# Attention's product with v in six parts, normalising one step later, and another order at its end

## The chip, the cores and the metric

The kernel runs on one core of one Trainium2 chip. A core has five engines that run at the same time, each through its own list of instructions in order: TensorE (PE in the profile, its weight loads PEld), VectorE (DVE), ScalarE (ACT), GpSimd (POOL), and SyncE (SP), which here only starts DMAs; ScalarE can start DMAs too. The metric is the device time of one execution in microseconds, as the median of several runs; lower is better.

## The reference

Attention with heads mixed before and after the softmax, and two dense blocks behind it:

```python
scores = scale * q @ k.T                                   # 4 batches, 12 heads, 448 x 448, depth 64
scores = einsum('bhij,hg->bgij', scores, w_pre)
attn = softmax(scores, axis=-1)                            # with + 1e-9 under the fraction
attn = einsum('bhij,hg->bgij', attn, w_post)
x = (attn @ v) as 1792 tokens x 768
x = ((x @ w1) * (x @ w2)) @ w3 @ w_out                     # 768 -> 1024 -> 1024 -> 768
out = relu(x @ w_in) ** 2 @ w_out2                         # 768 -> 2048 -> 768
```

The weights arrive as 64-bit numbers; those that are used must be turned into 32-bit ones on the chip.

## The kernel before

**Attention.** The queries of a batch are cut into four chunks (16 chunks `n` in all), a chunk into blocks of up to 10 queries times 12 heads (180 blocks `g`, `blocks`). The work goes in steps `d`, two blocks in each (`attention_step`). For a block: a DMA brings its scores together (`regroup`, tile `r`), two steps ahead; TensorE mixes the heads (`premix`, PSUM tile `sp`, two buffers); VectorE takes the row maximum (`rowmax`, tile `nm`); ScalarE the exponential and its sum (`expo`, tiles `p` and `sm`); GpSimd adds the small number to the sum (`norm_add`), VectorE inverts it (`norm_recip`); ScalarE writes the normalised upper half (`p_hi`, tile `ph`), VectorE the lower one (`p_lo`, tile `pl`); TensorE mixes the heads again (`tmix`, tile `tp`), two steps after `premix`; VectorE or ScalarE moves the result to `p2` (`p2_dve`, `p2_act`). When all blocks of a chunk are through, TensorE multiplies by v (`pv`, PSUM tile `pv`, one buffer) in two groups of 24 matmuls, ScalarE copies each result out (`pv_out`, tile `xs`), and a DMA stores it in `xd`. In the same steps the scores of the next chunk are made (`scores`, `evac`), and q and k are read and split in an upper and a lower part (`load_q`, `high_q`, `low_q`, `load_k`, `high_k`, `low_k`; k only at the start of a batch).

**What sets the order.** Nothing is scheduled by the compiler: instructions run on an engine as the code writes them. `attention_plan` gives the steps of scores, loads and `pv`; the tables `ORDER`, `NEEDS`, `LAG` and `AFTER` give the order inside a step and how many steps a kind lags behind `premix`.

**Weights ahead.** `Moe.ahead` turns 24 pieces of weights into 32 bits during attention: a load, a copy on ScalarE (`narrow`), three instructions on VectorE (`join`, tile `f`, lines 101, 103, 105), and a store. They are spread by a fixed period of three steps.

**The end of attention.** From step `closed` on there are no more scores; their memory is taken by the dense blocks. `tail_plan` reads the first eight weight pieces (`raw`) and x of the first batch (`xl`) and splits them (`wh`, `wl`, `xh`, `xl`); `early` gives TensorE the first matmuls of the dense blocks (`e`) between the last steps. `begin` and `Moe.step` read and split x of the second batch.

**Dense blocks.** Eight weight pieces lie ready at most, the others follow in a pipeline by pieces (`stage`: load, narrow, join, split); `mixed` is the order of the first units, `self.order` that of their matmuls. Pieces that were not turned ahead (`wide`) need the three joins here, and are stored again (`keep`).

## Time and profile before

| | us |
|---|---|
| runs shown | 1327.46, 1329.35, 1332.04 |
| median | 1329.35 |
| profiled execution | 1333.6 |
| its span | 1331.7 |
| until the first premix | 28.27 |
| first premix to the premix of step 83, the 84th | 402.27 |
| from there to the last wait of TensorE | 65.20 |
| from there to the end | 835.96 |

In a timeline row the first number is the start in microseconds, the second the length; `xN` is a number of instructions in one row, and brackets hold the idle time before and what ended it. A row of TensorE lasts until the result has left the array, so that rows overlap; what a step costs is read from start to start. The names are those of the tiles, without their numbers.

### The profile page before, as it was taken

What the parts mean: (1) busy time and instruction counts of PE and PEld (TensorE: products, weight loads), DVE (VectorE), ACT (ScalarE), POOL (GpSimd) and SP (SyncE); (2) the same over time, 40 slices, a digit from 0 to 9 for tenths busy, and PEclk for the clock granted to TensorE, in tenths of its full rate; (3) what the DMA queues carried; (4) which work ended last, traced back from release to release, by engine and by line L of the source; (5) the groups of instructions that cost most, each with busy time, mean ns of one, the idle gap of its engine ahead of it and who ended that gap; (6) DMA issues with size and microseconds to landing.
All of it is one profiled execution on the core that took longest, in us unless ns stands there. A gap on an engine that the chain in (4) does not pass through costs nothing.

```text
span 1331.7 us, 23506 instructions
## 1 busy us (share of the span) xinstructions
PE 1291.6 (97%) x8714; PEld 1117.5 (84%) x8714; DVE 839.9 (63%) x1414; ACT 727.0 (55%) x1558; POOL 469.6 (35%) x473
## 2 busy tenths in 40 slices
PE   6999999999999899999999999999999999999998
PEld 3667767776677579999999999999999999999998
DVE  4899889889888647585327785588345424801731
ACT  4878877887787644443323663574344434533530
POOL 4243234225211412200332232210468656734730
PEclk9999999999999899999999999999999999999999
DMA  5676567677564544565346764476321211121131
GB/s 182 199 207 218 158 211 221 194 196 229 171 177 138 168 127 123 159 207 158 107 147 204 253 205 148 136 209 237 105 74 55 72 60 42 66 72 37 57 98 58
DMA packets 109879, 196.03 MB, mean 147 GB/s; under 512 B 22405, under 2 KB 76677, under 8 KB 109317
## 3 DMA queue, kind: packets, MB, share of 16 engines
q1 hardware_dynamic: 93349, 176.86, 44.5%
q10 hardware_dynamic: 16416, 17.67, 3.7%
q8 instruction: 69, 1.13, 0.4%
q14 instruction: 45, 0.37, 0.1%
HBM read 120.18 MB, written 35.78 MB: 117 GB/s over the span
## 4 chain that ended last, share of the span: by engine, by line
PE 75%; issue 7%; ACT 6%; DVE 5%; DMA 4%; POOL 3%; SPq 0%; POOLq 0%; ACTq 0%; DVEq 0%
PE l L62 33%; PE y L62 9%; PE p L62 5%; PE sp L295 4%; PE tp L351 3%; PE pv L392 3%; ACT p L309 3%; PE sc L269 2%; DMA kraw<-k 1%; ACT ph L334 1%; POOL ql L252 1%; DVE p L366 1%; ACT s L280 1%; DVE nm L301 1%; POOL sm L324 1%
## 5 line engine op out<-in xcount | busy, mean ns | idle before, releaser
L295 PE MATMUL sp<-r,kpre 120*120 120x448 f32 x360 | 163.1, 575 | 14.1 <-ACT p L309 7.2
L309 ACT ACTIVATE p<-sp,nm 120x448 f32<-120x448 f32 x180 | 113.3, 637 | 73.1 <-DVE nm L301 72.1
L125 POOL TENSOR_TENSOR wl<-f,wh 128x384 fp32r<-128x384 f32 (+1 forms) x52 | 58.6, 1127 | 215.0 <-ACT wh L121 205.4
L351 PEld LDWEIGHTS <-ph 120*128 120x128 f16 (+1 forms) x1440 | 108.2, 99 | 30.7 <-issue 30.3
L324 POOL TENSOR_SCALAR sm<-sm 120x2 f32<-120x2 f32 (+3 forms) x94 | 29.5, 314 | 285.2 <-ACT p L309 282.2
L351 PE MATMUL tp<-kwh,ph 120*128 120x120 f16 x720 | 122.0, 219 | 4.5 <-ACT p L364 2.9
L301 DVE TENSOR_REDUCE nm<-sp 120x1 f32<-120x448 f32 x180 | 106.1, 618 | 27.4 <-PE sp L295 24.1
L341 DVE SCALAR_TENSOR_TENSOR pl<-p,sm,ph 120x448 f16<-120x448 f32 x180 | 122.7, 722 | 0.0
L334 ACT ACTIVATE ph<-p,sm 120x448 f16<-120x448 f32 x180 | 111.9, 683 | 18.2 <-DVE sm L329 17.9
L351 PE MATMUL tp<-kwh,pl 120*128 120x120 f16 x720 | 121.1, 218 | 0.0
L351 PE MATMUL tp<-kwl,ph 120*128 120x120 f16 x720 | 121.1, 218 | 0.0
L269 PE MATMUL sc<-kt,qh 128*110 128x448 f32 (+1 forms) x192 | 102.7, 535 | 9.8 <-DVE kt L230 8.3
L295 PEld LDWEIGHTS sp<-r,kpre 120*120 120x120 f32 x360 | 60.3, 188 | 59.0 <-issue 20.7
L280 ACT ACTIVATE s<-sc 110x448 f32<-110x448 f32 (+1 forms) x186 | 90.5, 554 | 14.2 <-PE sc L269 8.2
L366 DVE TENSOR_SCALAR p<-tp,iv 112x480 f32<-112x480 f32 (+1 forms) x135 | 90.9, 701 | 3.3 <-PE tp L351 3.2
L103 DVE SCALAR_TENSOR_TENSOR f<-y,f 128x384 int32<-128x384 int32 (+1 forms) x120 | 85.6, 713 | 4.1
L392 PE MATMUL pv<-p,v 112*64 112x110 f32 (+1 forms) x1536 | 80.7, 261 | 0.6 <-ACT xs L401 0.6
L269 PE MATMUL sc<-kt,ql 128*110 128x448 f32 (+1 forms) x192 | 76.1, 396 | 3.7 <-POOL ql L252 3.1
L105 DVE SCALAR_TENSOR_TENSOR f<-raw,f 128x384 int32<-128x384 int32 (+1 forms) x120 | 77.5, 646 | 3.3
L101 DVE TENSOR_SCALAR f<-y 128x384 int32<-128x384 int32 (+1 forms) x120 | 70.0, 583 | 14.4 <-ACT y L89 14.4
L392 PEld LDWEIGHTS pv<-p,v 112*64 112x64 f32 x1536 | 73.8, 137 | 4.0 <-ACT xs L401 0.8
L125 POOL TENSOR_TENSOR wl<-raw,wh 128x384 fp32r<-128x384 f32 (+1 forms) x36 | 44.2, 1231 | 92.1 <-ACT wh L121 92.1
(981 smaller groups left out, 3550.7 us busy)
## 6 DMA issues: line engine op xcount, KB each, us to landing
r<-s SPq DMA_DIRECT2D x172, 210.0 KB
raw<-w SPq DMA_DIRECT2D x32, 384.0 KB
raw<-win SPq DMA_DIRECT2D x32, 384.0 KB
raw<-wo SPq DMA_DIRECT2D x24, 512.0 KB
kraw<-k SPq DMA_DIRECT2D x22, 448.0 KB
raw<-w3t SPq DMA_DIRECT2D x16, 512.0 KB
qraw<-q SPq DMA_DIRECT2D x36, 220.0 KB
raw<-wo SPq DMA_DIRECT2D x16, 384.0 KB
```

Source lines behind the costliest of these rows:

```text
L62: nc.tensor.matmul(acc, w, x, start=(first and i == 0 and j == 0), stop=(last and i == n - 1 and j == 2), **kw)
L125: eng.tensor_tensor(self.out[i][1], self.ft.pop(i), f32(self.out[i][0]), ALU.subtract)
L269: nc.tensor.matmul(sc[:ic], t[:, hh * ic : hh * ic + ic], self.kt[b, h // 2][:, h % 2], start=(i == 0), stop=(i == 1))
L280: nc.scalar.activation(self.st[n][:ic, h], self.sc.pop((n, h))[:ic], AF.Copy)
L295: nc.tensor.matmul(t[:kk], self.kpre[:kk, :kk], self.rt.pop(g)[:kk], start=True, stop=True)
L301: nc.vector.tensor_reduce(nm[:kk], self.sp[g][:kk], AX.X, ALU.max, negate=True)
L309: nc.scalar.activation(p[:kk], self.sp.pop(g)[:kk], AF.Exp, bias=self.nm.pop(g)[:kk], accum_out=self.sm[g // 2][:kk, g % 2 : g % 2 + 1],)
L334: nc.scalar.activation(self.phl[g % NP][0][:kk, :S], self.pt[g][:kk], AF.Copy, scale=self.sm[g // 2][:kk, g % 2 : g % 2 + 1])
L341: nc.vector.scalar_tensor_tensor(l, self.pt.pop(g)[:kk], self.sm[g // 2][:kk, g % 2 : g % 2 + 1], h, ALU.mult, ALU.subtract)
L351: nc.tensor.matmul(t[:, j, :, :cnt], p[:kk, j * JP : j * JP + 128], w[:kk, :, :cnt], start=(i == 0), stop=(i == 2))
L366: nc.vector.tensor_scalar(d, t, self.iv[:JP], None, ALU.mult)
L392: nc.tensor.matmul(t[64 * e : 64 * e + 64, x, :ic], self.v[b][:, j, g], self.p2[n][:, j, g, :ic], start=(j == 0), stop=(j == JC - 1),)
```

## The change

`pv` is cut in six parts of 8 matmuls (`x` counts three of them to a group), spread over the steps until the next chunk is through, where before two groups of 24 stood in two steps; `pv_out` follows the third part of a group. `norm_recip` and `p_hi` lag one step; inside a step `p_hi` and `pv_out` stand first on ScalarE, `norm_recip` first on VectorE, and `p_lo` waits for `p_hi` of its step. `ahead` turns 20 pieces instead of 24, one join in a step, in steps that have no `high_k` and no `high_k` just before; `load_k` comes a step earlier, with three buffers. At the end: `p2_act` takes every second block; the loads of the first eight pieces and of x are started by ScalarE instead of SyncE; the lower halves of pieces and x are made by VectorE instead of GpSimd; x of the second batch is read and split earlier; the first matmuls of the dense blocks begin one block later. The first `l1` unit behind the early ones moves two pieces forward.

Two places on VectorE and ScalarE, in the middle of chunk 8. First VectorE before, from the row maximum of blocks 96 and 97 (`sm` numbers name the first block of a pair):

```order
L301 TENSOR_REDUCE nm96_3905<-sp96_3875 120x1
L301 TENSOR_REDUCE nm97_3907<-sp97_3877 120x1
L341 SCALAR_TENSOR_TENSOR pl2_93<-p94_3855,sm94_3854,ph2_92 120x448
L341 SCALAR_TENSOR_TENSOR pl3_95<-p95_3857,sm94_3854,ph3_94 120x448
L329 RECIPROCAL sm96_3911<-sm96_3911 120x2
L366 TENSOR_SCALAR p28_3863<-tp93_3892,iv_96 112x48x10
L245 CAST qh10_1_3921<-qraw10_1_3785 128x440
L301 TENSOR_REDUCE nm98_3977<-sp98_3937 120x1
L301 TENSOR_REDUCE nm99_3979<-sp99_3939 120x1
L341 SCALAR_TENSOR_TENSOR pl0_89<-p96_3912,sm96_3911,ph0_88 120x448
L341 SCALAR_TENSOR_TENSOR pl1_91<-p97_3914,sm96_3911,ph1_90 120x448
```

And the same place now:

```order
L329 RECIPROCAL sm94_3820<-sm94_3820 120x2
L301 TENSOR_REDUCE nm96_3883<-sp96_3844 120x1
L301 TENSOR_REDUCE nm97_3885<-sp97_3846 120x1
L341 SCALAR_TENSOR_TENSOR pl2_93<-p94_3821,sm94_3820,ph2_92 120x448
L341 SCALAR_TENSOR_TENSOR pl3_95<-p95_3823,sm94_3820,ph3_94 120x448
L366 TENSOR_SCALAR p28_3829<-tp93_3861,iv_96 112x48x10
L245 CAST qh10_1_3898<-qraw10_1_3755 128x440
L105 SCALAR_TENSOR_TENSOR f18_3835<-raw18_3602,f18_3835 128x384
L329 RECIPROCAL sm96_3889<-sm96_3889 120x2
L301 TENSOR_REDUCE nm98_3963<-sp98_3913 120x1
```

The reciprocal of a pair came behind its row maximum and the lower halves of the pair before; now it comes behind everything else of its step, ahead of the next row maximum. One join stands in a step.

ScalarE before, from the exponentials of blocks 94 and 95:

```order
L309 ACTIVATE p94_3855,sm94_3854<-sp94_3787,nm94_3848 120x448
L309 ACTIVATE p95_3857,sm94_3854<-sp95_3789,nm95_3850 120x448
L280 ACTIVATE s9_3493<-sc9_10_3791 110x448
L280 ACTIVATE s9_3493<-sc9_11_3794 110x448
L334 ACTIVATE ph2_92<-p94_3855,sm94_3854 120x448
L334 ACTIVATE ph3_94<-p95_3857,sm94_3854 120x448
L309 ACTIVATE p96_3912,sm96_3911<-sp96_3875,nm96_3905 120x448
L309 ACTIVATE p97_3914,sm96_3911<-sp97_3877,nm97_3907 120x448
L334 ACTIVATE ph0_88<-p96_3912,sm96_3911 120x448
L334 ACTIVATE ph1_90<-p97_3914,sm96_3911 120x448
L364 ACTIVATE p28_3863<-tp92_3879,iv_96 112x48x10
```

And now:

```order
L309 ACTIVATE p94_3821,sm94_3820<-sp94_3757,nm94_3811 120x448
L309 ACTIVATE p95_3823,sm94_3820<-sp95_3759,nm95_3813 120x448
L280 ACTIVATE s9_3457<-sc9_10_3761 110x448
L280 ACTIVATE s9_3457<-sc9_11_3764 110x448
L334 ACTIVATE ph2_92<-p94_3821,sm94_3820 120x448
L334 ACTIVATE ph3_94<-p95_3823,sm94_3820 120x448
L309 ACTIVATE p96_3890,sm96_3889<-sp96_3844,nm96_3883 120x448
L309 ACTIVATE p97_3892,sm96_3889<-sp97_3846,nm97_3885 120x448
L364 ACTIVATE p28_3829<-tp92_3848,iv_96 112x48x10
L89 ACTIVATE y20_3905<-raw20_3838 128x384
L334 ACTIVATE ph0_88<-p96_3890,sm96_3889 120x448
L334 ACTIVATE ph1_90<-p97_3892,sm96_3889 120x448
```

The order of exponential, copies and upper halves is kept; the copy of the mixed block (L364) and `narrow` (L89) now come ahead of the upper halves instead of behind them.

ScalarE at the end of attention before, from the upper halves of blocks 168 and 169:

```order
L334 ACTIVATE ph0_88<-p168_6658,sm168_6657 120x448
L334 ACTIVATE ph1_90<-p169_6660,sm168_6657 120x448
L364 ACTIVATE p214_6385<-tp164_6625,iv_96 112x48x10
L401 ACTIVATE xs13_1_6668<-pv13_1_6570 128x3x110
L665 ACTIVATE xh0_6533<-xl0_6534 128x6x110 x2
L309 ACTIVATE p170_6720,sm170_6719<-sp170_6683,nm170_6713 120x448
L309 ACTIVATE p171_6722,sm170_6719<-sp171_6685,nm171_6715 120x448
L334 ACTIVATE ph2_92<-p170_6720,sm170_6719 120x448
L334 ACTIVATE ph3_94<-p171_6722,sm170_6719 120x448
L121 ACTIVATE wh0_6731<-raw0_6612 128x384
L665 ACTIVATE xh0_6533<-xl0_6534 128x6x110
```

And at this end now, from the exponentials of blocks 166 and 167, with the DMA starts that ScalarE has taken from SyncE:

```order
L309 ACTIVATE p166_6549,sm166_6548<-sp166_6499,nm166_6539 120x448
L309 ACTIVATE p167_6551,sm166_6548<-sp167_6501,nm167_6541 120x448
L81 DMA raw0_6558<-w1f_60 128x384
L81 DMA raw1_6560<-w1f_60 128x384
L676 ACTIVATE xh0_6491<-xl0_6492 128x6x110
L334 ACTIVATE ph2_92<-p166_6549,sm166_6548 120x448
L334 ACTIVATE ph3_94<-p167_6551,sm166_6548 120x448
L309 ACTIVATE p168_6613,sm168_6612<-sp168_6567,nm168_6606 120x448
L309 ACTIVATE p169_6615,sm168_6612<-sp169_6569,nm169_6608 120x448
L364 ACTIVATE p214_6347<-tp164_6571,iv_96 112x48x10
L81 DMA raw2_6622<-w2f_61 128x384
L676 ACTIVATE xh0_6491<-xl0_6492 128x6x110
```

The split of x (`xh`) is spread over the steps, and each weight load and x load stands in ScalarE's list.

```diff
-        def load(self, i, src, wide):
+        def load(self, i, src, wide, eng=nc.sync):
             n = src.shape[1]
...
                 t = self.p.tile([128, PW, 2], I32, tag="raw", name=f"raw{i}", bufs=self.nraw)
-                nc.sync.dma_start(t[:, :n].rearrange("p n t -> p (n t)"), src.bitcast(I32))
+                eng.dma_start(t[:, :n].rearrange("p n t -> p (n t)"), src.bitcast(I32))
                 self.raw[i] = t[:, :n]
...
                 t = self.p.tile([128, PW], F, tag="raw", name=f"raw{i}", bufs=self.nraw)
-                nc.sync.dma_start(t[:, :n], src)
+                eng.dma_start(t[:, :n], src)
                 self.ft[i] = t[:, :n]
...
             else:
-                raw = self.ka.tile([128, 2, S], F, tag="kraw", name=f"kraw{b}_{r}", bufs=2)
+                raw = self.ka.tile([128, 2, S], F, tag="kraw", name=f"kraw{b}_{r}", bufs=3)
             nc.sync.dma_start(raw, k[b, :, 2 * r : 2 * r + 2])
...
         def p2_act(self, g):
-            if g % 4 == 0:
+            if g % (4 if g < first[15] - 4 else 2) == 0:
                 self.p2_evac(g, 0)
...
         def p2_dve(self, g):
-            if g % 4:
+            if g % (4 if g < first[15] - 4 else 2):
                 self.p2_evac(g, 1)
...
-        def pv(self, n, y):
+        def pv(self, n, y, x):
             b, c = divmod(n, 4)
...
             assert all(("p", z) in self.done for z in range(first[n], first[n + 1]))
-            t = self.pvt[n, y] = self.ps.tile([128, 3, IC], F, tag="pv", name=f"pv{n}_{y}", bufs=1)
-            for x in range(3):
-                for j in range(JC):
-                    for e in range(2):
-                        g = 6 * y + 2 * x + e
-                        nc.tensor.matmul(
-                            t[64 * e : 64 * e + 64, x, :ic], self.v[b][:, j, g], self.p2[n][:, j, g, :ic],
-                            start=(j == 0), stop=(j == JC - 1),
-                        )
-        def pv_out(self, n, y):
+            if x == 0:
+                self.pvt[n, y] = self.ps.tile([128, 3, IC], F, tag="pv", name=f"pv{n}_{y}", bufs=1)
+            t = self.pvt[n, y]
+            for j in range(JC):
+                for e in range(2):
+                    g = 6 * y + 2 * x + e
+                    nc.tensor.matmul(
+                        t[64 * e : 64 * e + 64, x, :ic], self.v[b][:, j, g], self.p2[n][:, j, g, :ic],
+                        start=(j == 0), stop=(j == JC - 1),
+                    )
+        def pv_out(self, n, y, x):
+            if x < 2:
+                return
             o, ic, _ = CHUNKS[n % 4]
...
                         add(t - 2, "high_q", n, h // 4)
-            for y in range(2):
-                add((first[n + 1] + 5 + (5 if n < 15 else 0) * y) // 2, "pv", n, y)
+            t0, t1 = (first[n + 1] + 5) // 2 + (n == 14), (first[n + 2] if n < 15 else 0) // 2 + 2
+            for z in range(6):
+                add(t0 + z * (t1 - t0) // 6 if n < 15 else t0, "pv", n, *divmod(z, 3))
         for b in range(1, B):
...
                 t = lo[4 * b] - 6 + 3 * r // 2
-                add(t - 1, "load_k", b, r)
+                add(t - 2, "load_k", b, r)
                 add(t, "high_k", b, r)
...
         ("premix", "scores", "tmix", "pv"),
-        ("expo", "evac", "p_hi", "p2_act", "pv_out"),
-        ("rowmax", "p_lo", "norm_recip", "p2_dve", "high_q", "high_k"),
+        ("p_hi", "pv_out", "expo", "evac", "p2_act"),
+        ("norm_recip", "rowmax", "p_lo", "p2_dve", "high_q", "high_k"),
         ("norm_add", "low_q", "low_k"),
...
     NEEDS = {
-        "rowmax": "premix", "expo": "rowmax", "evac": "scores", "norm_add": "expo", "norm_recip": "norm_add",
-        "p_hi": "norm_recip", "p2_act": "tmix", "p2_dve": "tmix",
+        "rowmax": "premix", "expo": "rowmax", "evac": "scores", "norm_add": "expo", "p_hi": "norm_recip", "p_lo": "p_hi",
+        "p2_act": "tmix", "p2_dve": "tmix",
     }
...
         "premix": 0, "tmix": 2, "p2_act": 2, "p2_dve": 2, "rowmax": 0, "expo": 0,
-        "norm_add": 0, "norm_recip": 0, "p_hi": 0, "p_lo": 1,
+        "norm_add": 0, "norm_recip": 1, "p_hi": 1, "p_lo": 1,
     }
...
             wop = [self.wo_piece(c, h) for c in range(8) for h in range(2)]
-            mixed, rest = l1[:4] + wop[:6], wop[6:]
+            mixed, rest = l1[:4] + wop[:4] + [l1[4]] + wop[4:6], wop[6:]
             for i in range(8):
-                mixed.append(l1[4 + i])
+                mixed += [l1[4 + i]] if i else []
                 for _ in range(1 + (i % 4 == 3)):
...
             self.at = [int(x) for x in n]
-            self.order = [None, (3, 0), (0, 1), None, (1, 1), None, (2, 1), None, (3, 1)]
-            for i in range(10, len(self.units)):
+            self.order = [None, (3, 0), (0, 1), None, (1, 1), None, (2, 1), None, (3, 1), (8, 0), (8, 1)]
+            for i in range(11, len(self.units)):
                 self.order += [(i, t) if self.units[i][1] else None for t in range(len(self.units[i][0]))]
...
-        def ahead(self, ka, n, start, period):
+        def ahead(self, ka, n, plan, last):
             w, ev = Weights(ka, PW, 2, 2, 2, 0, 0), {}
-            def at(d, f):
-                ev.setdefault(d, []).append(f)
+            keys = {d for d, x in plan.items() if "high_k" in x}
+            free = [d for d in range(1, last) if not {d, d - 1} & keys]
+            at = lambda d, f: ev.setdefault(d, []).append(f)
...
+            ends = [-9, -9]
             for j, i in enumerate([i for i, x in enumerate(self.pieces) if "keep" in x][:n]):
-                d, x = start + period * j, self.pieces[i]
-                at(d, lambda i=i, src=x["src"]: w.load(i, src, True))
-                at(d + 2, lambda i=i: w.narrow(i))
-                for part in range(3):
-                    at(d + 3 + part // 2, lambda i=i, part=part: w.join(i, part))
-                at(d + 6, lambda i=i, dst=x["keep"]: store(i, dst))
+                x, parts = self.pieces[i], [free[(3 * j + k) * len(free) // (3 * n)] for k in range(3)]
+                at(max(parts[0] - 5, ends[j] + 1), lambda i=i, src=x["src"]: w.load(i, src, True))
+                at(parts[0] - 1, lambda i=i: w.narrow(i))
+                for k, d in enumerate(parts):
+                    at(d, lambda i=i, k=k: w.join(i, k))
+                at(parts[2] + 2, lambda i=i, dst=x["keep"]: store(i, dst))
+                ends.append(parts[2])
                 self.pieces[i] = {"src": x["keep"], "wide": False}
...
-            for i in range(11):
-                t = 1 + i if i < 8 else 13 + i
-                at(t, lambda i=i: w.load(i, self.pieces[i]["src"], self.pieces[i]["wide"]))
-                if i == 8:
-                    at(t + 4, lambda i=i: w.narrow(i))
-                if i < 8:
-                    at(t + 4, lambda i=i: (w.place(i), w.high(i), w.rest(i)))
+            for i in range(8):
+                t = 2 * i if i > 3 else (1, 2, 4, 5)[i]
+                at(t, lambda i=i: w.load(i, self.pieces[i]["src"], False, nc.scalar))
+                at(2 * i + 5, lambda i=i: (w.place(i), w.high(i)))
+                at(2 * i + 7, lambda i=i: w.rest(i, nc.vector))
             for u in range(4):
-                at(u - 1, lambda u=u: self.load_x(u))
-                at(u + 3, lambda u=u: self.split_x(u))
+                at(u // 2 - 1, lambda u=u: self.load_x(u, nc.scalar))
+                at(2 * u + 2, lambda u=u: self.high_x(u))
+                at(2 * u + 4, lambda u=u: self.low_x(u, nc.vector))
             return ev
...
             self.load_x(4)
+            self.load_x(6)
+            for i in (8, 9, 10):
+                self.w.load(i, self.pieces[i]["src"], True)
+            self.w.narrow(8)
             slots = []
...
                     self.wot[c, h] = slots[4 * c + 2 * h], slots[4 * c + 2 * h + 1]
-            for u in (5, 6, 7):
-                self.load_x(u)
             for i in range(3):
...
         def step(self, p, it):
-            if p == 1:
+            if p == 0:
                 for u in range(4, 8):
-                    self.split_x(u)
+                    self.high_x(u)
+                    self.low_x(u, nc.gpsimd if u == 5 else nc.vector)
...
-        def load_x(self, u):
+        def load_x(self, u, eng=nc.sync):
             t, u4 = divmod(u, 4)
...
                 w = slice(CHUNKS[u4][0], sum(CHUNKS[u4 + 1][:2]))
-                nc.sync.dma_start(f32(self.xy["x", t][1][:, :, w]), xd[t, :, :, w])
-        def split_x(self, u):
+                eng.dma_start(f32(self.xy["x", t][1][:, :, w]), xd[t, :, :, w])
+        def x_rows(self, u):
             t, u4 = divmod(u, 4)
             o, ic, _ = CHUNKS[u4]
-            xh, xl = (x[:, :, o : o + ic] for x in self.xy["x", t])
+            return tuple(x[:, :, o : o + ic] for x in self.xy["x", t])
+        def high_x(self, u):
+            xh, xl = self.x_rows(u)
             nc.scalar.activation(xh, f32(xl), AF.Copy)
-            eng = nc.gpsimd if u < 4 or u == 5 else nc.vector
+        def low_x(self, u, eng):
+            xh, xl = self.x_rows(u)
             eng.tensor_tensor(xl, f32(xl), f32(xh), ALU.subtract)
...
         M, tail = Moe(), {}
-        ahead = M.ahead(ka, 24, 4, 3)
+        ahead = M.ahead(ka, 20, ev, closed - 3)
         for d in step:
...
                     a()
-                for _ in range(1 if g >= nb - 5 else 0):
+                for _ in range(1 if g >= nb - 4 else 0):
                     next(heads, None)
```

## Rows read from the trace of the kernel before

**Rows 1.** Windows, all engines: busy us (count) of each, granted clock, DMA share, GB/s; four stages.
```profile
0.00:28.27 28.27, 16.33 (x37) 9.04 (x37) 11.34 (x20) 13.81 (x21) 15.07 (x23) 1.00 0.55 176
28.27:430.54 402.27, 386.92 (x3923) 281.41 (x3923) 352.08 (x675) 320.88 (x760) 126.73 (x165) 0.99 0.66 195
430.54:495.74 65.20, 56.41 (x561) 44.15 (x558) 37.46 (x63) 35.66 (x79) 20.21 (x21) 0.92 0.50 147
495.74:1331.70 835.96, 831.95 (x4199) 782.92 (x4199) 439.05 (x658) 356.62 (x699) 307.61 (x264) 1.00 0.40 123
```

**Rows 2.** Timeline of TensorE, 209 to 240 us: start, length, instruction, count.
```profile
209.66 1.72 PE L295 MATMUL sp<-r,kpre 120*120 120x448 f32 x4
...
213.39 2.48 PE L392 MATMUL pv<-p,v 112*64 112x110 f32 x48
215.80 1.76 PE L295 MATMUL sp<-r,kpre 120*120 120x448 f32 x4
...
234.57 1.72 PE L295 MATMUL sp<-r,kpre 120*120 120x448 f32 x4
...
238.63 1.71 PE L295 MATMUL sp<-r,kpre 108*108 108x448 f32 x4
```

**Rows 3.** Timeline of TensorE around the last attention step with scores before it.
```profile
427.68 1.76 PE L295 MATMUL sp<-r,kpre 120*120 120x448 f32 x4
...
430.54 0.97 PE L295 MATMUL sp<-r,kpre 120*120 120x448 f32 x2
```

**Rows 4.** Waits in 28 to 430 us: who waited for whom, us in total, times, longest.
```profile
ACT p L309 <- DVE nm L301: 68.7, 51, 4.0
...
PEld sp L295 <- ACT p L309: 19.0, 39, 2.3
...
DVE sm L329 <- POOL sm L324: 9.4, 16, 1.5
...
PE sp L295 <- DMA r<-s: 2.7, 2, 1.8
```

**Rows 5.** Timeline of VectorE in one step, 210 to 216 us.
```profile
210.39 1.31 DVE L366 TENSOR_SCALAR p<-tp,iv 112x480 f32<-112x480 f32 x2
211.63 0.37 DVE L245 CAST qh<-qraw 128x440 fp32r<-128x440 f32 x1
211.92 0.61 DVE L221 CAST kt<-kraw 128x896 fp32r<-128x896 f32 x1
...
212.84 0.56 DVE L103 SCALAR_TENSOR_TENSOR f<-y,f 128x384 int32<-128x384 int32 x1
213.31 1.15 DVE L301 TENSOR_REDUCE nm<-sp 120x1 f32<-120x448 f32 x2
214.38 1.27 DVE L341 SCALAR_TENSOR_TENSOR pl<-p,sm,ph 120x448 f16<-120x448 f32 x2
```

**Rows 6.** Windows, 545 to 570 us, where the two weight pieces in question are used.
```profile
545.00:570.00 25.00, 24.73 (x124) 22.88 (x123) 16.00 (x28) 11.27 (x22) 5.05 (x5) 1.00 0.55 171
```

**Rows 7.** Windows, 434 to 442 us, while x is read back.
```profile
434.00:442.00 8.00, 5.63 (x82) 4.36 (x78) 5.04 (x10) 5.10 (x13) 0.59 (x2) 0.97 0.81 193
```

**Rows 8.** Timeline of all engines, 442 to 457 us; idle time before in brackets.
```profile
442.55 3.31 PE L295 MATMUL sp<-r,kpre 120*120 120x448 f32 x4 [2.92 <-DMA r<-s]
...
445.07 0.63 ACT L309 ACTIVATE p<-sp,nm 120x448 f32<-120x448 f32 x1 [1.11 <-DVE nm L301]
...
448.06 1.23 ACT L334 ACTIVATE ph<-p,sm 120x448 f16<-120x448 f32 x2 [0.77 <-DVE sm L329]
...
450.53 2.70 DVE L341 SCALAR_TENSOR_TENSOR pl<-p,sm,ph 120x448 f16<-120x448 f32 x2
...
456.04 0.17 DVE L329 RECIPROCAL sm<-sm 120x2 f32<-120x2 f32 x1 [2.82 <-POOL sm L324]
```

**Rows 9.** Timeline, 475 to 496 us: a DMA issue on ScalarE, and TensorE's last wait.
```profile
481.44 0.40 ACTq L403 DMA_DIRECT2D xd<-xs  x1
...
495.74 0.44 PE L62 MATMUL l<-xl,wh 128*128 128x448 f32 x1 [1.47 <-DVE xl L667]
```

## Prediction

> **What bounds the kernel now.** I read the windows by stage first, then the timeline of TensorE inside attention, then the waits, then the timeline of the end.
>
> The windows [rows 1] give four stages. In the last one, 835.96 us long, TensorE is busy for 831.95: it is the bound and nothing in this change gives it less to do. In attention up to step 83 (402.27 us) it is busy for 386.92, VectorE for 352.08, ScalarE for 320.88. That sum hides something: a row of TensorE lasts until its result has left the array, so I build the floor from starts. A step without scores or pv goes from 427.68 to 430.54, 2.86 us: two premix and 24 tmix [rows 3]. From 234.57 to 238.63 is 4.06, the same with six scores, so a score (two matmuls) costs (4.06 - 2.86)/6 = 0.20. From 209.66 to 215.80 is 6.14, with four scores and one pv group of 48 passes: 6.14 - 2.86 - 0.80 = 2.48 for the group, of which 2.41 would be its passes and 0.07 the seam, an estimate [rows 2]. Steps 0 to 82 hold, by the order, 81 steps with tmix, two without (1.6 each, estimate), 350 scores and 27 groups: 231.7 + 3.2 + 70.0 + 67.0 = 371.8. The trace needs 402.27, so 30.5 us are lost there.
>
> To whom? The only wait of TensorE named by the page itself is 2.7 us for a regrouped block and 19.0 for the exponential to free a premix buffer; the big row above them, the exponential waiting 68.7 us in 51 waits for the row maximum, points further back [rows 4]. The row maximum is VectorE's, and VectorE's list is in order. I counted its instructions in each step by the order and gave them the durations of [rows 5]: 0.575 for a row maximum, 0.635 for a lower half, 0.655 for a copy to `p2`, 0.37 and 0.61 for the casts of q and k, 0.56 for a join, and an estimate of 0.1 for the reciprocal. Over 83 steps that is 354 us against 373 of TensorE's passes, so on average VectorE keeps up; in 39 of the steps it doesn't, and what it has too much of in those sums to 33.9 us. Step 31 is an example: TensorE needs 2.86, VectorE 2 x 0.575 + 2 x 0.635 + 2 x 0.655 + 0.37 + 0.61 + 2 x 0.56 + 0.1 = 5.9. The step before has 6.17 of TensorE because it holds a pv group. Only two premix buffers stand between the engines, so little of an imbalance is carried over.
>
> The third stage [rows 1] is 65.20 us at a granted clock of 0.92. Its floor: seven steps of 2.86, 24 more tmix (2.5, estimate), five pv groups (12.4), 54 early matmuls at 0.20 (10.8) and 19 that the phase behind would else do (3.8), 49.8 in all; 15.4 are lost.
>
> **The change part by part.**
>
> *The middle.* The same count over the new order: step 31 has 3.75 of TensorE (one part of pv) and 2 x 0.575 + 2 x 0.635 + 2 x 0.655 + 0.37 + 0.61 + 0.1 = 4.8 of VectorE; the joins are gone from it. Over 83 steps VectorE falls to 348 us (four pieces fewer, 12 joins of 0.56), steps in which it has more than TensorE go from 39 to 24, and their overhang from 33.9 to 16.5: 51% of it goes. I apply that share to the loss less the 2.7 that is a DMA's: 27.8 x 0.51 = 14.2 less. Against it stand seams: the pieces of pv in these steps go from 27 to 68, 41 x 0.07 = 2.9 more. Sum -11.3. Bounds: none of the loss goes (+2.9), all of it goes (2.9 - 27.8 = -24.9). I take the share, since the count explains a loss of the size that the trace has (33.9 against 27.8).
>
> *Reciprocal and upper halves a step later.* The row "VectorE's reciprocal waits for GpSimd", 9.4 us in 16 waits, goes [rows 4]: the addition of GpSimd now has the rest of a step. What it brings is inside the sum above. What is queued behind: on ScalarE, in its list, the upper halves of a pair (1.23, [rows 8]) stand directly ahead of the next two exponentials, as before, but wait for a reciprocal that is now behind all else in VectorE's step. So the exponential starts no earlier than reciprocal + 1.23, and the second of a pair ends about 2.5 us after the reciprocal (1.23 + 2 x 0.63). TensorE needs the first buffer back a step later: 402.27/83 = 4.85 us before, some 4.7 by the sum above. VectorE needs 348/83 = 4.2 on average, so the reciprocal stands on average before the premix of its step is done, and TensorE's step hides it: cost 0. Without that cover it is rival A.
>
> *Copies at p2, key loads.* Counts of `p2_dve` and `p2_act` in the middle are the same; the third `kraw` buffer and an earlier issue can take only part of the loss that the joins beside key casts share. Counted above, nothing added.
>
> *The end.* Three of its losses have rows. Step 85's premix waits 2.92 for its block [rows 8] while the DMA engines are at 0.81 with x and weights [rows 7], and 442.55 to 448.06 takes 5.5 against 2.86, another 2.6, at the lower clock that follows the wait. Now ScalarE starts ten of these loads, so that SP's list holds the regroup alone, and x and weights come at other steps: I take half of the 5.5, -2.8, as the same bytes still move in the same few steps. VectorE waits 2.82 for GpSimd's addition, behind lower halves of x and weights on GpSimd [rows 8]; with these on VectorE that wait goes, and about 0.3 more of the chain behind it: -3.1. VectorE pays for it with eight lower halves of weights and seven of x, each about a microsecond or less at the rate of `pl` [rows 5]; its free time here is 65.20 - 37.46 = 27.7 us [rows 1]. And TensorE's last wait, 1.47 for `xl` of the second batch [rows 9], with 0.5 of small waits beside it: those splits come earlier now, -1.3 of the 2.0. Five parts of pv where two groups stood: +0.5 with the starts of DMAs on ScalarE (10 x 0.40, [rows 9], hidden in its 65.20 - 35.66 = 29.5 us of free time, but for one in front of an exponential). Sum -6.7. Bounds: nothing goes and all 4.0 of the starts lie on the path, +4; all of the lost 15.4 goes, -15.
>
> *The dense stage.* The four pieces that are no longer turned ahead cost it 12 joins, 12 x 0.56 = 6.7 us of VectorE, and four copies and four stores. They are `l1[10]` and `l1[11]`, used near 545 to 570; there VectorE is busy 16.0 of 25 us [rows 6], so 9 lie free under TensorE. I take +0.5; bounds 0 and +6.7. The stage as a whole is 835.96 and stays.
>
> *Sum.* -11.3 - 6.7 + 0.5 = -17.5. The profiled execution took 1333.6 (span 1331.7, 1.9 outside), 4.25 over the median of 1329.35; the sum is made on its own span and taken from the median: 1329.35 - 17.5 = 1312.
>
> The term for the block late in step 85 is one on which a page speaks. [Rows 7] show 0.81 of the DMA engines' time taken at that place. The Trainium skill, "DMA: Bandwidth & Descriptors", section "Issuing engines are not separate DMA queues", says that DMAs started from several engines land on the same 16 DMA engines, and only the time of starting them is saved. By that alone moving the starts to ScalarE would bring nothing there, and the sum would be 2.8 less of a gain, 1315. The loads are also spread over other steps, which this rule doesn't speak of, so I keep the half.
>
> **Rivals.**
>
> *A: the upper halves hold up the exponentials.* For it: ScalarE runs in order, the reciprocal has moved to the end of VectorE's step, and 39 times already TensorE waits for an exponential [rows 4]. If VectorE is late by a step's worth of overhang, the reciprocal is late, then upper halves, exponentials, premix, row maximum, and the lateness runs in a ring. Price: 39 waits each longer by one exponential, 0.63 [rows 8], +24.6; with seams +2.9, the end -6.7 and +0.5: 1329.35 + 21.3 = 1351. It decides where the reciprocal comes over 2.1 us after its step's premix starts (4.7 less 1.23, 0.63 and a seam or two of semaphores) in most steps; against it, 59 steps of 83 have VectorE lighter than TensorE now.
>
> *B: the middle's losses aren't VectorE's load.* For it: over this stage the DMA share is 0.66 and the granted clock 0.99 [rows 1], so late loads and slower stretches can sit in some of the lost steps; against it, the ranking of [rows 4]. Then the gain only cancels the seams, 0, and the end, which shares that cause, gives -4 + 0.5: 1326.
>
> *C: all of it goes.* -24.9, -10.6 at the end (its named losses, 5.5 + 3.1 + 2.0), +0.5: 1294. For it: the joins stood together where the key casts stood, and a stall also brings the lower clock, so that smoothing pays twice. Against it, 24 steps still have too much of VectorE.
>
> *D: the dense stage pays.* All 6.7 of the joins on the path: 1329.35 - 18.0 + 6.7 = 1318. Against it the 9 free microseconds of [rows 6].
>
> **How the numbers follow.** Forecast 0.50 (its own range 1304 to 1321), A 0.13, B 0.20, C 0.12, D 0.05. A measurement of this kernel can tell about 0.3% from no change, 4.0 us: same is 1325.4 to 1333.3. All of the forecast, C and D are faster, 0.67, and of B (around 1326) nearly half, 0.09: 0.76. Same: half of B, 0.11, and 0.01 of A. Slower: A, 0.12. The range leaves out one half of C below and A above: 1297 to 1333.
>
> **What would show it.** Right: from the first premix to that of step 83 about 391 us, steps near their floor with a loss of some 19 in all; no wait of the reciprocal for GpSimd; fewer waits of TensorE's premix for the exponential; steps that hold a pv part between 3.7 and 5.4 us where 2.9 and 6.2 stood side by side; the third stage about 58.5; the last about 836 with no wait for `wh` or `wl`. The exponential's wait for the row maximum may fall or stay, it is not itself time. Wrong: exponentials that start right behind upper halves which waited for the reciprocal, with TensorE waiting for them (A); lost steps at the same places, with waits for `r`, `kraw` or `qraw` (B); TensorE waiting for weights near 545 to 570 (D).

## The result and the profile after

The changed kernel takes 1314.76 us (median of 4 runs, 1314.67 to 1316.07) against 1328.4 (4 runs, 1326.57 to 1332.04): ratio 0.9896, 95% interval 0.9873 to 0.9919. That is 1.0% less, and clear of the scatter. 1312 was forecast. The profiled execution after has a span of 1312.9, and with 1.9 around it lies on the median; that of before lay some 5 us above its own, so the spans differ by 18.8 us and the medians by 13.6.

The windows of the changed kernel, at the same four places as [rows 1] (busy us and count of PE, PEld, DVE, ACT, POOL; granted clock, DMA share, GB/s):

```profile
0.00:27.14 27.14, 14.28 (x36) 7.65 (x37) 10.83 (x20) 13.93 (x21) 15.08 (x23) 0.81 0.62 204
27.14:423.08 395.94, 389.91 (x3923) 280.91 (x3922) 343.98 (x665) 320.98 (x758) 140.66 (x166) 1.00 0.65 191
423.08:478.14 55.06, 52.06 (x559) 41.62 (x558) 36.40 (x66) 35.59 (x78) 7.75 (x8) 1.00 0.51 160
478.14:1312.90 834.76, 830.36 (x4199) 781.61 (x4199) 447.04 (x673) 359.46 (x705) 307.05 (x264) 1.00 0.41 126
```

Of the 18.8 us the middle gives 6.3 (402.27 to 395.94), the end of attention 10.1 (65.20 to 55.06), the dense stage 1.2, the beginning 1.1. The waits of the middle, 28 to 430 us (who waited for whom: us, times, longest):

```profile
ACT ph L334 <- DVE sm L329: 62.0, 56, 2.6
...
ACT p L309 <- DVE nm L301: 6.8, 8, 3.9
...
PEld sp L295 <- ACT p L309: 5.2, 9, 1.7
```

ScalarE's big wait of [rows 4] has only moved from the exponential to the upper half: 68.7 us there, 62.0 here. It is not itself time: TensorE does not stand still for all of it. Nearer to time is the third row, TensorE's wait for the exponential: 19.0 before, 5.2 now.

The timeline of TensorE shows what a part of pv costs:

```profile
119.46 1.73 PE L393 MATMUL pv<-p,v 112*64 112x110 f32 x32
121.12 1.76 PE L295 MATMUL sp<-r,kpre 120*120 120x448 f32 x4
...
124.07 0.97 PE L393 MATMUL pv<-p,v 112*64 112x110 f32 x16
124.98 1.77 PE L295 MATMUL sp<-r,kpre 120*120 120x448 f32 x4
```

The step from 121.12 to 124.98 takes 3.86: with no scores in it, 2.86 for the bare step [rows 3] and 1.00 for a part of 16 passes (each of its 8 matmuls stands in the trace as two). A group of 48 took 2.48 [rows 2]. So a pass is (2.48 - 1.00)/32 = 0.046 us, and a seam, what a part costs beside its passes, is 0.26, not the 0.07 of the forecast. With these I give every step a floor; what a stage takes above it is "lost". In the table "end" goes from the premix of step 83 to TensorE's last wait, "rest" from there on:

| kernel | median us | ratio to before, interval | steps 0 to 82 | of it lost | end | rest |
|---|---|---|---|---|---|---|
| before | 1328.4 to 1330.5 | 1 | 402.3 | 30.5 | 65.2 | 836.0 |
| before_again (second trace) | one run, 1332.3 | | 403.1 | 31.3 | 64.9 | 834.4 |
| changed | 1314.8 | 0.9896 (0.9873-0.9919) | 395.9 | 13.5 | 55.1 | 834.8 |
| pv_two | 1318.2 | 0.9916 (0.9900-0.9931) | 397.3 | 25.5 | 55.9 | 835.2 |
| pv_four | 1316.4 | 0.9904 (0.9889-0.9919) | 396.2 | 17.3 | 55.0 | 835.3 |
| old_joins | 1322.1 | 0.9944 (0.9929-0.9959) | 402.5 | 20.1 | 54.9 | 834.4 |
| no_lag_2 | 1314.4 | 0.9888 (0.9875-0.9902) | 392.7 | 10.2 | 56.8 | 835.1 |
| start_5 | 1316.4 | 0.9904 (0.9889-0.9918) | 398.4 | 15.9 | 55.0 | 834.8 |
| old_tail | 1317.6 | 0.9917 (0.9901-0.9933) | 396.3 | 13.8 | 56.7 | 834.8 |
| out_first | 1320.1 | 0.9936 (0.9917-0.9954) | 391.3 | 19.5 | 63.7 | 834.4 |
| store_act | 1325.7 | 0.9967 (0.9955-0.9978) | 396.3 | 24.5 | 65.2 | 834.4 |
| four_12n | 1317.1 | 0.9915 (0.9896-0.9934) | 387.7 | 8.9 | 56.5 | 842.6 |
| pv_three | 1375.6 | 1.0346 (1.0330-1.0363) | 450.4 | 74.2 | 60.4 | 834.8 |
| no_lag | 1386.2 | 1.0427 (1.0403-1.0451) | 460.3 | 77.8 | 65.1 | 835.1 |

The intervals come mostly from the kernel before, whose runs scatter over 7 us, and each ratio is to runs of before made beside it. Between two variants some 2 us apart they overlap; there I lean on the traces, where the same steps are late or not. A trace is one execution: steps 1 to 4, the same in five of the changed kernels, lose 5.4 to 7.3 in them.

### The profile page after: what moved, and what is told of

Same layout as the page of the kernel before. It is cut to its first block, busy times and chain, and to the rows that moved or that the text cites. A ratio compares the mean times of both kernels' runs of the same rounds, so it can differ in the third digit from the quotient of the medians.

```text
span 1312.9 us, 23462 instructions
## 1 busy us (share of the span) xinstructions
PE 1286.6 (98%) x8714; PEld 1111.8 (85%) x8714; DVE 838.2 (64%) x1422; ACT 730.0 (56%) x1562; POOL 470.5 (36%) x461
## 4 chain that ended last, share of the span: by engine, by line
PE 91%; issue 2%; ACT 2%; DVE 2%; DMA 1%; POOL 1%; SPq 0%; ACTq 0%; POOLq 0%; DVEq 0%
PE l L62 33%; PE sp L295 10%; PE y L62 9%; PE tp L351 7%; PE pv L393 6%; PE sc L269 5%; PE p L62 5%; PE e L62 1%; DMA qraw<-q 1%; POOL ql L252 1%; ACT p L309 1%; PE 8.40000000000006_2_13294 L62 1%; PE 66.4000000000002_3_14236 L62 1%; PE 8.40000000000006_3_13312 L62 1%; PE 8.40000000000006_0_13022 L62 1%
## 5 line engine op out<-in xcount | busy, mean ns | idle before, releaser
L295 PE MATMUL sp<-r,kpre 120*120 120x448 f32 x360 | 159.6, 566 | 4.8 <-ACT p L309 3.7
L324 POOL TENSOR_SCALAR sm<-sm 120x2 f32<-120x2 f32 (+3 forms) x94 | 43.5, 463 | 277.8 <-ACT p L309 268.5
L125 POOL TENSOR_TENSOR wl<-f,wh 128x384 fp32r<-128x384 f32 (+1 forms) x56 | 62.6, 1117 | 224.5 <-ACT wh L121 214.8
L301 DVE TENSOR_REDUCE nm<-sp 120x1 f32<-120x448 f32 x180 | 109.1, 619 | 38.2 <-PE sp L295 30.2
L269 PE MATMUL sc<-kt,qh 128*110 128x448 f32 (+1 forms) x192 | 99.9, 521 | 10.9 <-DVE kt L230 8.3
L393 PE MATMUL pv<-p,v 112*64 112x110 f32 (+1 forms) x1536 | 90.8, 264 | 0.6 <-ACT xs L404 0.6
L269 PE MATMUL sc<-kt,ql 128*110 128x448 f32 (+1 forms) x192 | 73.5, 383 | 2.9 <-POOL ql L252 2.8
L89 ACT ACTIVATE y<-raw 128x384 f32<-128x384 f32 (+1 forms) x120 | 70.5, 587 | 9.5 <-DMA raw<-wo 5.2
```

The costliest lines, as they stand in the source:

```text
L269: nc.tensor.matmul(sc[:ic], t[:, hh * ic : hh * ic + ic], self.kt[b, h // 2][:, h % 2], start=(i == 0), stop=(i == 1))
L295: nc.tensor.matmul(t[:kk], self.kpre[:kk, :kk], self.rt.pop(g)[:kk], start=True, stop=True)
L301: nc.vector.tensor_reduce(nm[:kk], self.sp[g][:kk], AX.X, ALU.max, negate=True)
L393: nc.tensor.matmul(t[64 * e : 64 * e + 64, x, :ic], self.v[b][:, j, g], self.p2[n][:, j, g, :ic], start=(j == 0), stop=(j == JC - 1),)
```

## The experiments

**One part undone at a time**

pv in two groups a chunk:

```diff
-                add(t0 + z * (t1 - t0) // 6 if n < 15 else t0, "pv", n, *divmod(z, 3))
+                t = t0 + z * (t1 - t0) // 6 if n == 14 else (first[n + 1] + 5 + 5 * (z // 3)) // 2
+                add(t if n < 15 else t0, "pv", n, *divmod(z, 3))
```

> The changed kernel with pv in two groups of 24 matmuls again, at the steps where they stood before (chunks 0 to 13); all else as changed. In the trace of the changed kernel a part of 16 passes adds 1.00 us to a step (3.86 against 2.86), where two groups of 48 added 2.48 each: 0.046 a pass and 0.26 a seam. 41 seams less are 10.7 us less of TensorE's own time. Theory (steps in which VectorE has more work than TensorE lose the difference): that overhang goes from 15.2 to 29.8 us by the counted order, and the loss over the floor was 0.9 of it, so +13; sum +2.5, 1317. Rival (the loss went because of the joins, the lag and the loads; the spread of pv pays nothing): only the seams, 1304.

1318.2, within 1 us of the theory: 10.7 us of seams gone, 12.0 more lost (25.5 against 13.5), and 0.9 at the end. The places are not those of the theory: 6.8 of the 12.0 stand in the 27 steps that hold a group, 5.2 in the 56 others. And TensorE waits for another engine in them. Its row for the lower half of q, 28 to 430 us (2.2 in 3 waits in the changed kernel):

```profile
PE sc L269 <- POOL ql L252: 11.1, 15, 1.3
```

In all 15 places GpSimd starts on this half right behind its addition to the sum, which in 13 of them had waited for an exponential; the upper half had been cast at least 3.2 us before. One of them:

```profile
219.91 0.38 DVE L245 CAST qh<-qraw 128x440 fp32r<-128x440 f32 x1
...
220.45 1.23 ACT L334 ACTIVATE ph<-p,sm 120x448 f16<-120x448 f32 x2 [2.05 <-DVE sm L329]
...
222.20 0.62 ACT L309 ACTIVATE p<-sp,nm 120x448 f32<-120x448 f32 x1
...
223.06 0.68 POOL L324 TENSOR_SCALAR sm<-sm 120x2 f32<-120x2 f32 x1 [1.79 <-ACT p L309]
...
223.82 1.13 POOL L252 TENSOR_TENSOR ql<-qraw,qh 128x440 fp32r<-128x440 f32 x1
...
225.00 0.45 PE L269 MATMUL sc<-kt,ql 128*110 128x448 f32 x1 [0.70 <-POOL ql L252]
```

So the size is that of the count, but the lateness reaches TensorE through the order on ScalarE and GpSimd. The lower half of q ahead of the addition wasn't tried.

The joins as before (24 pieces, `M.ahead(ka, 24, 4, 3)` with its fixed period):

> The changed kernel with the weights turned ahead as before: 24 pieces, a piece every three steps, two joins in one step and one in the next. Theory of the load per step: overhang 18.6 instead of 15.2 us, +3.1, and up to 1 us less in the dense stage: 1317. Rival (the joins beside the key casts made the large losses): the lost steps near 180, 315 and 347 us come back, 3 to 5 us each, 1325. Rival (joins don't matter when pv is spread): 1314.

1322.1, between theory and rival. From step 9 on it loses 15.5 us where the changed kernel loses 4.9; the count had 15.0 against 9.3. The loss lies spread in steps of 0.4 to 1.2 us, not at the places the rival named, and the wait for the lower half of q has grown here too, from 2.2 to 7.1 in 13 waits. In steps 0 to 7 it loses less, 4.5 against 8.5.

Reciprocal and upper halves in the step of the exponential, by `ORDER`, `NEEDS` and `LAG` of before:

```diff
-        ("p_hi", "pv_out", "expo", "evac", "p2_act"),
-        ("norm_recip", "rowmax", "p_lo", "p2_dve", "high_q", "high_k"),
+        ("expo", "evac", "p_hi", "p2_act", "pv_out"),
+        ("rowmax", "p_lo", "norm_recip", "p2_dve", "high_q", "high_k"),
...
-        "norm_add": 0, "norm_recip": 1, "p_hi": 1, "p_lo": 1,
+        "norm_add": 0, "norm_recip": 0, "p_hi": 0, "p_lo": 1,
```

> The changed kernel with the order inside a step of before: reciprocal and upper half in the step of the exponential, exponentials first on ScalarE. Theory of the load per step: VectorE's and TensorE's work per step are the same (overhang 15.2 both), so 0 to +3 us, 1315 to 1318, although VectorE waits for GpSimd's addition again (9 us in some 16 waits). Rival (the lag is what took the losses away): the premix's waits for the exponential come back, 19.0 instead of 5.2 us, and with them some 10 us: 1325. Third: the lag costs at the start (steps 1 to 4 lose 4.3 us more than before, the reciprocal is queued behind the cast of a late q), and without it the time is 1311.

1386.2: far outside all three. The waits of TensorE, 28 to 430 us, name the reason:

```profile
PE pv L393 <- ACT xs L404: 40.6, 16, 5.9
```

There is one pv tile. A first part of the second group stands a step behind the last of the first, and with `pv_out` last on ScalarE the copy that frees the tile came too late. The experiment had moved two things. So again, with `pv_out` alone put first:

```diff
+        ("pv_out", "expo", "evac", "p_hi", "p2_act"),
```

> The changed kernel with reciprocal and upper half in the step of the exponential as before, but with pv_out first in each step on ScalarE as changed (in no_lag it had gone last, and TensorE waited 41 us in 16 waits for the one pv tile to be copied out). It parts two things that no_lag moved together. Theory (no_lag's 71 us were the pv tile's): the load per step is that of the changed kernel, 1315 to 1318. Rival (the lag itself is what carries the gain): the premix's waits for the exponential, 19.0 us before and 5.2 after, come back: 1325 or more.

1314.35, the same as the changed kernel: the lag gives nothing in the median. And 72 us lie between `pv_out` last (no_lag) and first. The middle is even 3.2 us shorter in the trace, 2.4 of it in steps 1 to 4, and the end 1.8 longer.

**Other cuts of pv**

Three parts of 16 matmuls (`z // 2 * (t1 - t0) // 3`):

> The changed kernel with pv in three parts of 16 matmuls a chunk, at even distances. Theory: 27 seams less than with six parts, of 0.26 each, -7.0, against an overhang of VectorE of 19.3 instead of 15.2 us, +3.7: -2.5 to -3.3, 1312. Rival (seams alone): 1308. If the even load matters more than the count says: 1316 or more.

1375.6, outside both, for the reason of `no_lag`: its middle part crosses from the first group to the second in one step, and the copy between stands a step later on ScalarE. Waits of TensorE, 28 to 430 us:

```profile
PE pv L393 <- ACT xs L404: 34.2, 12, 3.8
```

Four places that never cross (`(0, 0, 1, 2, 2, 3)[z] * (t1 - t0) // 4`):

> The changed kernel with the six parts of pv in four places of a chunk (two, one, two, one) instead of mostly five, never across the two groups, so that no part waits for the pv tile (pv_three put the last part of a group and the first of the next in one step, and TensorE waited 34 us in 12 waits). Theory (seam 0.26 against overhang of VectorE): 14 seams less, -3.6; overhang 16.6 instead of 15.2, +1.3: 1312.5. Rival (one part a step is what keeps VectorE and ScalarE even): 1316.

1316.4, the rival's number: in the middle the 3.6 us of seams saved come back as 3.9 of loss.

**The start**

Joins from step 5 on (`range(5, last)`):

> The changed kernel with the first join in step 5 instead of step 1. In the trace of the changed kernel steps 1 to 4 lose 5.9 us, 4.3 more than before, behind a cast of q that waits 2.0 us for its load and has the reciprocal behind it; with the joins of before (none until step 7) steps 1 to 4 lose 2.8. Theory (loads and joins of the weights in the first steps cause it): -3, 1311.5. Rival (the reciprocal's new place behind the cast causes it alone): 1315. The 60 joins stand a little closer in the rest, overhang after step 9 the same, 9.3.

1316.4: later joins alone don't help. Steps 1 to 4 still lose 5.5 us. Waits from 30 to 50 us:

```profile
ACT ph L334 <- DVE sm L329: 6.2, 2, 4.1
...
DVE qh L245 <- DMA qraw<-q: 4.2, 1, 4.2
...
PE sp L295 <- DMA r<-s: 3.3, 1, 3.3
```

The cast of q waits 4.2 us for its load, and behind it, on VectorE, stands the reciprocal for which ScalarE waits 4.1; TensorE itself waits 3.3 for a block. Without the lag (no_lag_2) the same steps lose 3.4, which speaks for rival A of the prediction, in four steps of 83. But the lag alone isn't it: old_joins keeps it, loses 2.8 in these steps, and no cast waits for q in them. There the first weight load starts at 45.98 us; here one still starts at 29.89, ahead of two regroups and a load of q:

```profile
29.89 0.53 SPq L77 DMA_DIRECT2D raw<-w  x1
```

So start_5 tested the joins of its theory and not the loads, and old_joins speaks for the loads. How much each does wasn't parted.

**The end**

Loads, lower halves, x, p2 copies and the first dense units of before:

> The changed kernel with the end of attention of before: loads on SyncE, lower halves on GpSimd, x of the second batch late, p2 copies one in four on ScalarE, order of the first dense units of before. Theory by the traces: from the premix of step 83 to TensorE's last wait took 65.2 before and 55.1 after, so +10, 1325. Rival (half of those 65.2 was the one profiled execution of before, which took 5 us more than the median; step 85's wait of 2.92 for its block and the lower clock behind it): +5, 1320. Both should show in this trace: whether the premix waits for r at the end again.

1317.6, below even the rival's number. Its end takes 56.7 us, not 65.2. So 8.5 of the 10.1 us at the end don't come from what was changed there. From what they come wasn't parted: the end is also 55 to 57 us in pv_two, pv_four, old_joins and no_lag_2, which all keep `pv_out` first and pv of chunk 14 in parts.

**What was left of before**

> The kernel before, unchanged, for a second trace. The first one took 1333.6 us, 5 over the median, and its end (premix of step 83 to TensorE's last wait) 65.2 us, 2.92 of it a premix waiting for its block and 2.6 the lower clock behind it. If that wait belongs to the kernel, it stands here too, and the end takes 62 to 66. If it was that execution's own, the end takes 57 to 60 and the span is some 1327.

The end takes 64.9, with 2.8 before the premix of step 85 again (named there after ScalarE's copy to `p2`, not the block): the first trace of before was no accident. The same steps lose, but not the same amounts: the nine steps named under store_act lose 12.0 in the first trace and 8.4 here, steps 1 to 4 lose 1.6 and 3.7.

One word of before moved:

```diff
-        ("expo", "evac", "p_hi", "p2_act", "pv_out"),
+        ("pv_out", "expo", "evac", "p_hi", "p2_act"),
```

> The kernel before with one word moved: pv_out first in each step on ScalarE instead of last; all else as before. In the trace of before SyncE's list stands 117.7 us in 28 waits for that copy (71.3 in 29 after the change), with the store at its head and the regroup of later blocks behind it. Theory (the late blocks at the end come from this store): no wait of 2.9 for r in step 85, the end some 5 to 6 us shorter, in the middle 0 to -2: 1323. Rival (late x and weights on the same DMA engines make the block late): end unchanged, 1329. Rival (the copy ahead of the exponentials delays them): 1331 or more.

1320.1, 9 us of the whole 13.6, but not where I had looked for it: the middle gives 11.0 in the trace, the end 1.5. So in the middle this one word does more than the whole change: 391.3 against 395.9 (this trace lies 1.3 us below its median). The rest of the change wins at the end, 55.1 against 63.7. How it works is seen in the timeline of before around step 66, which took 8.8 us:

```profile
341.77 2.48 PE L392 MATMUL pv<-p,v 112*64 112x110 f32 x48
...
344.09 1.73 SPq L287 DMA_DIRECT2D r<-s  x2
...
349.27 0.43 ACT L401 ACTIVATE xs<-pv 128x330 f32<-128x330 f32 x1
...
349.73 0.39 SPq L403 DMA_DIRECT2D xd<-xs  x1
...
350.21 1.69 SPq L287 DMA_DIRECT2D r<-s  x2
...
353.32 0.34 SPq L238 DMA_DIRECT2D qraw<-q  x1
...
355.83 0.66 PE L295 MATMUL sp<-r,kpre 108*108 108x448 f32 x1 [1.77 <-DMA r<-s]
355.85 0.55 ACT L280 ACTIVATE s<-sc 110x448 f32<-110x448 f32 x1 [3.89 <-DMA qraw<-q]
```

pv is done at 344.25, its copy is made at 349.27, because ScalarE has it last in its list. SyncE's list has the store of that copy (L403) at its head from 345.82 on, and behind it the regroup of the next blocks and a load of q. The regroup starts 3.9 us late by that, and the load of q comes behind it; TensorE waits for the block, and ScalarE for scores whose q came late. With `pv_out` first:

```profile
333.62 2.48 PE L392 MATMUL pv<-p,v 112*64 112x110 f32 x48
...
337.03 0.46 ACT L401 ACTIVATE xs<-pv 128x330 f32<-128x330 f32 x1
...
337.52 0.39 SPq L403 DMA_DIRECT2D xd<-xs  x1
...
338.00 1.72 SPq L287 DMA_DIRECT2D r<-s  x2
```

The waits of engines for loads, 28 to 430 us, in before, 17.1 us in all:

```profile
DVE qh L245 <- DMA qraw<-q: 6.5, 8, 2.0
...
ACT s L280 <- DMA qraw<-q: 3.9, 1, 3.9
DVE kt L221 <- DMA kraw<-k: 3.5, 3, 1.4
...
PE sp L295 <- DMA r<-s: 2.7, 2, 1.8
...
ACT s L280 <- DMA r<-s: 0.5, 1, 0.5
```

In before_again they come to 22.5. In out_first the trace has no such row in that stretch. To tell the store from the earlier copy itself, the store alone was taken out of SyncE's list, `pv_out` left last:

```diff
-            eng = nc.sync if n < 15 else nc.scalar
+            eng = nc.scalar
```

> The kernel before with one thing changed: the stores of pv's results are started by ScalarE, right behind the copy, in all chunks (before: by SyncE, the last chunk by ScalarE). pv_out stays last in its step on ScalarE. In the trace of before PE, VectorE and ScalarE wait 17 us for loads of q, k and r in 28 to 430 us; with pv_out first (out_first) none is left. Theory (the store at the head of SyncE's list, waiting for the copy, holds the loads behind it): these waits go here too, and the time is that of out_first, 1320, give or take 2 for 30 starts of 0.40 us on ScalarE. Rival (it is the earlier copy itself, through ScalarE's order or the pv tile): the waits for loads may go or stay, the time stays at 1327 to 1329.

1325.7: faster than before (0.9967), but only half of what was expected. The waits for loads are gone but for 1.3 us on VectorE and as much on ScalarE. VectorE's rows, 28 to 430 us:

```profile
DVE sm L329 <- POOL sm L324: 18.5, 25, 1.5
...
DVE qh L245 <- DMA qraw<-q: 1.3, 1, 1.3
```

and so is the loss of the steps that carried them: steps 24, 25, 32, 33, 48, 55, 56, 66 and 67, which lose 12.0 us in before and 8.4 in before_again, lose 2.5 here and in out_first. So the held loads are shown as a cause. The 5 us by which store_act then loses more than out_first stand mostly in other steps (12, 18, 40, 49, 57, 63), with VectorE waiting 18.5 us for the sum where it waited 9.4. Whether the 0.40 us starts on ScalarE or the late copy does that wasn't parted.

**A try for a faster one**

no_lag_2 with pv in four places and 12 pieces ahead:

> A try for a faster one: no_lag_2 with pv in four places a chunk and 12 instead of 20 weight pieces turned ahead. Theory (load per step): 14 seams of 0.26 less, -3.6; VectorE's overhang after step 8 is 8.4 instead of 9.3 us, so no more is lost in the steps than in no_lag_2; the dense stage takes 8 more pieces, 24 joins of 0.56 = 13.4 us on VectorE, beside TensorE: 0 to +3. Sum 1311 to 1314 (no_lag_2 1314.35). Rival (steps without pv lose because VectorE is late in them whatever the mean, as in pv_four): 1315 to 1316. Rival (dense weights late): TensorE waits for wh or wl between 490 and 600 us, 1318 or more.

1317.1, the third case, just under its number. Attention loses only 8.9 us, but the dense stage takes 842.6. Waits of TensorE, 490 to 600 us:

```profile
PE p L62 <- DVE wl L125: 3.2, 1, 3.2
PE l L62 <- POOL wl L125: 1.4, 3, 0.5
PE l L62 <- ACT wh L121: 1.0, 1, 1.0
```

This is rival D, with 12 wide pieces more than before where the change has four. None of the runs beats the changed kernel by more than can be measured.

## Why the prediction was right, and where it was not

The total came out near by luck, with terms that were wrong against each other, and the stated range of 1297 to 1333 holds the kernel before as well.

**The middle: two sizes wrong, against each other.** -11.3 was forecast, -6.3 came. The term for seams, 41 x 0.07 = 2.9, was mis-sized: 0.26 each, 10.7. It was taken from one size of group, which can't part passes from seam. The loss fell by 17.0, not 14.2.

**The cause of the loss was half named.** The step "27.8 x 0.51, since the count explains a loss of the size that the trace has" gave all of it to VectorE's load. For that load speaks that pv_two came out within 1 us of what the count gave, and that old_joins loses in the direction of the count, by more; against it, that TensorE waits there mostly for GpSimd's half of q, a row that the prediction passed over in before too, 28 to 430 us: `PEld sc L269 <- POOL ql L252: 11.7, 18, 0.9`. And 11.0 of the 30.5 go when one copy is made earlier, with VectorE busy for 352 us as before. The count for out_first is that of before, 33.9, and it loses 19.5: that the count had the size of the loss was chance. The prediction's own example shows it: step 31, with 5.9 of VectorE against 2.86, takes 3.02 in before, so it loses 0.16. Steps 32 and 33 behind it lose 4.6 together in the first trace of before, 2.5 in the second, and 1.8 in out_first, with the same joins.

The prediction has no term for `pv_out` being first on ScalarE. It put it at nothing without a reason, and it is 9 us from before. Rival B, late data, was right on that part of the cause and wrong on its result, since the change cures it. The row was there, among SyncE's own waits. In 28 to 430 us it stands like this in before

```profile
SPq L403 <- ACT xs L401: 100.1, 25, 7.3
```

and like this in out_first:

```profile
SPq L403 <- ACT xs L401: 37.3, 18, 4.9
```

The rest of what was done in the middle made it no shorter than that in the traces: from step 8 on the changed kernel loses 10.4 us less than out_first and pays 10.7 for seams, and its first steps lose 4.3 more.

**The end: -6.7 forecast, -10.1 measured, with other reasons.** "I take half of the 5.5, as the same bytes still move": the wait for the block goes whole, and it goes in out_first and store_act too, where x and weights are still loaded by SyncE at the old steps; step 84 takes 2.86 there, 5.94 before. It was SyncE's order, neither the DMA engines' share of 0.81 [rows 7], which is 0.96 and 0.87 at the same place in these two, nor who starts the loads. But the end as a whole takes 63.7 and 65.2 in them: what the block gave is lost again in steps 86 and 87. The rule of the Trainium skill that the prediction weighed ("DMA: Bandwidth & Descriptors", "Issuing engines are not separate DMA queues") isn't contradicted: the starts on ScalarE were not what helped. It speaks of where DMAs run; what these runs show is what one start that waits does to those behind it in an engine's list. VectorE's wait for GpSimd at 425 to 470 us, 5.9 in before, has two cures in the change. With the lag and the lower halves still on GpSimd (old_tail):

```profile
DVE sm L329 <- POOL sm L324: 1.2, 1, 1.2
```

with the lower halves on VectorE and no lag (no_lag_2):

```profile
DVE sm L329 <- POOL sm L324: 2.9, 5, 1.2
```

and with neither (out_first) 10.4. So taking one away shows little. Of the last wait 1.41 us are still there, where 1.3 was to go.

**The lag was costed at 0 and is 0** in the median, though for a reason the prediction didn't have: it costs 2.4 us in the first steps, where a late load holds the reciprocal (rival A) as long as weights are loaded early, and gives 1.8 at the end.

**The dense stage** was costed at +0.5 and came out 1.2 shorter, within the 1.6 us between two traces of before. Four wide pieces more are hidden; twelve are not.

**The sum** came near, by luck, because the seams' 7.8 us too little were met by 2.8 more of loss gone, 3.4 at the end, 1.7 in the dense stage and 1.1 before the first premix; the trace gave -18.8 where -17.5 was said. That the medians give 13.6 is the last step's fault: a sum made on an execution 4.25 us above its median was taken from the median whole. Whether part of what the change removed lay in what made that execution long isn't shown: both traces of before are of executions above the median.

**In its working** three things don't hold, and none moves the sum: 0.20 us is the price of one matmul of the scores, not of two (the 350 are matmuls); the terms of the floor of the end add up to 49.5, not 49.8; and the 19 that were to be lost hold the 2.9 of seams.

Undoing one part costs, in medians, 3.4 (pv), 7.3 (joins) and 2.8 (end), by the ratios to before 2.7, 6.4 and 2.8; `pv_out` first gives 9 from before. These add to more than 13.6: the parts cover for one another, as the two cures for GpSimd's wait do.

What stays open: what shortens the end by 8.5 us, and whether `pv_out` first with the new end alone would beat the whole change. Steps 0 to 7 lose 8.5 us in the changed kernel and 4.2 before; with the weights ahead as before it is 4.5 (old_joins), but whether their loads, copies or joins do it wasn't parted. A third buffer for k and its earlier load weren't tried alone.

## What to carry to other kernels

Read the DMA queue's own waits beside the engines': a store that waits for a late copy holds every load behind it, and what shows on the engines is casts, row maxima and matmuls that are late for other reasons. Before splitting a group of matmuls, take its price from two sizes, so that the seam is known; here the seams ate what the split saved in the middle, and where the tile between the parts was freed late (no_lag, pv_three) it cost 60 us and more. A count of each engine's work by step that matches the loss in size doesn't yet name its cause: look at what TensorE waits for in the steps that lose. When several edits cure one wait, undoing them singly understates each.

## What was not expected of the hardware

A seam between pv and its neighbours on TensorE costs 0.26 us at a granted clock of 1.00, as much as 5.6 of its own passes of 0.046. And the scatter of runs differs by kernel: four runs each spread over 5.5 us in before, 1.4 in the changed kernel, 0.6 in pv_four and 7.5 in no_lag. Why isn't shown.
